# Phi units of a fused retention and two-MoE kernel: loaded in the experts' order, one expert ahead

## The chip, the cores and the metric

One Trainium2 chip, one core, one program. The metric is the device time of one execution in microseconds (us). All data are fp32; the large matrix products run as sums of two reduced parts (fp32r).

## The reference

```python
# attention: B,H,S,D = 4,8,768,64; x is its output as 3072 tokens x 512
for t in range(S):
    state = gamma * state + outer(k[:, :, t], v[:, :, t])
    y[:, :, t] = scale * (q[:, :, t] @ state)
# first MoE: 8 experts, each token goes to one
logits = x @ w_gate;  e_idx = argmax(logits)
gate_w = softmax(logits)[e_idx];  eom = sigmoid(x @ w_output_gate)
for e in range(8):
    mask = e_idx == e
    h = relu(x[mask] @ w1[e])                       # 512 -> 1024
    out[mask] = gate_w[mask] * eom[mask, e] * (h @ w2[e])
# second MoE: soft slots, 8 experts x 4 slots
logits = out @ phi                                  # 3072 x 32
d = softmax(logits, over tokens);  c = softmax(logits, over slots)
slot_in = d.T @ out;  slot_out = expert MLP of each slot
return c @ slot_out                                 # 3072 x 512
```

## The kernel before

The kernel runs as three stages in one hand-written order (the schedule is manual: every engine executes its instructions in the order of the program, and SP's queue issues nearly all loads in that order too).

**First stage** (pool scope `pa`, lines 311 to 757): 24 tiles of 128 tokens (`NTILE`). A loop over i runs the steps named in `ORDER`: score matmuls of tile i+1 (L452), masks on VectorE (L462), output matmuls (L476, L485), state (L499), and for every third tile the gates of three tiles (L535, L550), their choice of expert and their rank. `load(i + 4)` (L420) reads 1 MB of raw q, k, v into a pool of five buffers. `x_put` and `scale_put` (L648, L640) write finished rows and their scales to `xs` in DRAM.

**Phi units.** The logits of the second MoE are needed while the first MoE runs. Instead of multiplying the first MoE's output by phi, the kernel multiplies `w2[e] @ phi` once per expert: 8 experts x 4 units (`NQ` = 32). A unit is 512 KB of w2, 4 matmuls (8 instructions) against a 32-column block of phi (L237); after four units VectorE transposes the block (L407, L1107). Units 0 to 15 run inside the first stage's loop (step `w`), loaded through a pool of four buffers (L377); 16 to 23 run in its tail (`u1`, `u3`, L700), loaded as four 1 MB pieces into the raw buffers (L382); 24 to 31 are loaded at the start of the second stage (L1101) and run in two groups behind its steps 2 and 4. They run in the order of the expert's number, ahead of the time at which it is known in which order the experts are processed, so each finished block goes to DRAM (`wps`, L245) and comes back by the ordered expert's number (L943).

**The turn.** After the last tile, the counts give the order of the experts by size; SP reads the first expert's number (`load_er(0)`) and loads its first weights (L214); the token lists are made (L731), and GpSimd gathers the rows of the first expert from `xs` (L743). Then all engines read a limit and branch over a block for overflowing experts (L857, not entered with these inputs).

**Second stage** (lines 878 to 1222): 64 steps g, expert e = g // 8, part f = g % 8. A step is `l1(g)`, 12 matmuls (L921), with the weights split in two two steps ahead (`split_w`, L223, L224) and loaded three steps ahead (`load_w`, three buffers). `behind(e - 1, f)` places the other work of the previous expert behind the steps: logits (L957), their sum, softmax parts, slot products (L1040, L1062), combine weights (`c_exp`, `c_put`), w2 loads. Rows of the next expert are gathered at f = 0 to 3, scaled at f = 4 and 5, transposed at f = 7 (L899). In free buffers the weights of the second MoE (`m2`) are loaded ahead: 50 of 128 tiles (`NPRE`).

**Third stage** (lines 1225 to 1358): the second MoE on 32 slots: first layer (L1238), second layer in two column halves (L1275, order `ORDC`), then the output as `c @ slot_out`: the first half's columns of all tokens (`emit_out(0)`, parts `o0-4` to `o20-24`), then the second half's (`emit_out(1)`). `combine` (`s`, `S`) finishes a half's sum. Each output DMA writes two tokens' half rows per partition, 1 KB pieces. Remaining m2 tiles are loaded as buffers fall free.

Of the kernel before, what the change touches and what calls it, by code (L numbers as in the profile page):

```python
# [36 lines left out]
NPRE, NX = 50, 4  # L37
NH = 6
NQ = 4 * E
NQL, NQ0 = 16, 24  # L40
# [98 lines left out]
def retention_moe_kernel(ctx, tc, qt, kt, kn, vn, gates, moe_w1, moe_w2,  # L139
# [30 lines left out]
    wps = dr.tile([E, 128, KF * NS], F32, name="wps")  # L170
# [57 lines left out]
    wtt, wacc, wput, wput_old = {}, {}, {}, []  # L228

    def wq_mm(u, pool, tag):  # L230
        if not 0 <= u < NQ:
            return
        e, kk = divmod(u, 4)
        if kk == 0:
            wacc[e] = pool.tile([128, 256], F32, tag=tag, name="wps")
        for g, t in enumerate(wtt.pop(u)):
            nc.tensor.matmul(out=wacc[e][32 * g:32 * g + 32, :], lhsT=phi[:, kk, :], rhs=t,  # L237
                             start=(kk == 0), stop=(kk == KD - 1), skip_group_check=True)

    def wq_put(wait):  # L240
        for e in list(wput):
            if wait and e not in wput_old:
                wput_old.append(e)
                continue
            nc.sync.dma_start(out=wps[e], in_=wput.pop(e).rearrange("p f s -> p (f s)"))  # L245
# [65 lines left out]
    with ExitStack() as pa:  # L311
        sc2 = pa.enter_context(tc.tile_pool(name="sc2", bufs=2))
        io = pa.enter_context(tc.tile_pool(name="io", bufs=5))
# [55 lines left out]

        wst = pa.enter_context(tc.tile_pool(name="wst", bufs=4))  # L370

        def wq_load(i):

            if i % 5 < 4 and i // 5 * 4 + i % 5 < NQL:
                e, q = divmod(i // 5 * 4 + i % 5, 4)
                t = wst.tile([128, FF], F32, tag="wt", name="wt")
                nc.sync.dma_start(out=t, in_=moe_w2[1, e, :, q * FF:(q + 1) * FF])  # L377
                wtt[4 * e + q] = [t[:, g * 256:g * 256 + 256] for g in range(4)]
            elif NTILE - 4 <= i < NTILE:
                e, q = divmod(NQL + 2 * (i + 4 - NTILE), 4)  # L380
                t = io.tile([128, 4 * DM], F32, tag="raw", name="wt2")
                nc.sync.dma_start(out=t, in_=moe_w2[1, e, :, q * FF:(q + 2) * FF])  # L382
                for h in range(2):
                    wtt[4 * e + q + h] = [t[:, h * FF + g * 256:h * FF + g * 256 + 256] for g in range(4)]

        def wq_at(i):
            if 2 <= i < 22 and (i - 2) % 5 < 4:
                return [(i - 2) // 5 * 4 + (i - 2) % 5]
            return []

        def wq_step(i):
            for u in wq_at(i):
                wq_mm(u, pT, "w")
                wq_turn(u)

        wq_end = iter(range(NQL, NQ0))

        def wq_next(n):
            for _ in range(n):
                u = next(wq_end)  # L400
                wq_mm(u, pT, "w" if u < NQL + 4 else "st")

        def wq_turn(u):
            if u % 4 == 3 and 0 <= u < NQ0:

                wput[u // 4] = pd[:, 0:KF, :] if u == NQ0 - 1 else sc2.tile([128, KF, NS], F32, tag="ws", name="ws")
                nc.vector.transpose(out=wput[u // 4], in_=wacc.pop(u // 4).rearrange("p (f t) -> p f t", t=32))  # L407
# [309 lines left out]
        for g in range(3):  # L717
            load_w(g)
# [159 lines left out]
    with ExitStack() as pb:  # L878
# [231 lines left out]
        for u in range(NQ0, NQ0 + 4):  # L1110

            first = wq_early(u)
            if u == NQ0:
                after(first, gets[0])
# [270 lines left out]
```

## Time and profile before

| | us |
|---|---|
| median of three runs | 433.23 (432.98 to 437.45) |
| the profiled execution | 433.41 |
| its span, first to last instruction | 431.6 |
| TensorE (PE) busy | 378.8 (88%) |
| VectorE (DVE) busy | 259.4 (60%) |
| ScalarE (ACT) busy | 161.1 (37%) |
| GpSimd (POOL) busy | 110.0 (25%) |

The DMA engines moved 132.96 MB, 308 GB/s on average. The time beyond the span, 1.8 us, lies around the program. Busy shares are averages over three stages with different limits, so they are read by stage.

### The profile page before, as it was taken

What the parts mean: (1) busy time and instruction counts of PE and PEld (TensorE: products, weight loads), DVE (VectorE), ACT (ScalarE), POOL (GpSimd) and SP (SyncE); (2) the same over time, 40 slices, a digit from 0 to 9 for tenths busy, and PEclk for the clock granted to TensorE, in tenths of its full rate; (3) what the DMA queues carried; (4) which work ended last, traced back from release to release, by engine and by line L of the source; (5) the groups of instructions that cost most, each with busy time, mean ns of one, the idle gap of its engine ahead of it and who ended that gap; (6) DMA issues with size and microseconds to landing.
All of it is one profiled execution on the core that took longest, in us unless ns stands there. A gap on an engine that the chain in (4) does not pass through costs nothing.

```text
span 431.6 us, 11452 instructions
## 1 busy us (share of the span) xinstructions
PE 378.8 (88%) x4398; PEld 285.7 (66%) x4398; DVE 259.4 (60%) x676; ACT 161.1 (37%) x359; POOL 110.0 (25%) x117
## 2 busy tenths in 40 slices
PE   2799998797981999999999999999999996799990
PEld 2776776676750877877897878878788873224560
DVE  1468988589774326658666586675756756414350
ACT  1242222122211237454654646445554441112242
POOL 2223321222113131214324253152431312020020
PEclk9899999899995699999999999999999999899996
DMA  8999999999998797896877958778687688999998
GB/s 268 380 412 321 345 356 345 382 361 340 331 334 219 287 334 275 288 326 195 275 277 257 332 187 293 263 251 301 223 290 244 201 285 292 393 398 404 398 371 285
DMA packets 68290, 132.96 MB, mean 308 GB/s; under 512 B 10660, under 2 KB 31138, under 8 KB 65410
## 3 DMA queue, kind: packets, MB, share of 16 engines
q1 hardware_dynamic: 61442, 120.17, 80.1%
q0 software_dynamic: 3344, 8.34, 5.8%
q10 hardware_dynamic: 3440, 3.63, 2.5%
q8 instruction: 36, 0.59, 0.5%
q14 instruction: 28, 0.23, 0.2%
HBM read 117.89 MB, written 14.25 MB: 306 GB/s over the span
## 4 chain that ended last, share of the span: by engine, by line
PE 63%; DMA 16%; DVE 11%; ACT 3%; issue 2%; another core or an unknown queue 2%; SPq 1%; ACTq 1%; POOL 0%; POOLq 0%; DVEq 0%
PE hps L921 28%; PE gps L1040 5%; PE fh L1238 4%; PE s L452 3%; PE o L485 3%; DMA raw<-in_qt_dram 3%; PE so L1275 3%; DMA r<-in_moe_w_dram 3%; DMA wt<-in_moe_w_dram 3%; PE xps L899 3%; PE slo L1062 2%; PE lps L957 2%; DMA xs<-xr 2%; DMA raw<-in_vn_dram 2%; PE o L476 2%
## 5 line engine op out<-in xcount | busy, mean ns | idle before, releaser
L921 PE MATMUL hps<-xh,wh 128*128 128x416 f32 (+2 forms) x256 | 92.6, 362 | 1.1 <-ACT h L932 1.1
L921 PE MATMUL hps<-xl,wh 128*128 128x416 f32 (+2 forms) x256 | 89.8, 351 | 0.1
L921 PE MATMUL hps<-xh,wl 128*128 128x416 f32 (+2 forms) x256 | 89.6, 350 | 0.0
L224 DVE TENSOR_TENSOR wl<-r,wh 128x512 fp32r<-128x512 f32 x64 | 43.7, 684 | 52.9 <-ACT wh L223 43.8
L921 PEld LDWEIGHTS hps<-xh,wh 128*128 128x128 f32 x256 | 48.7, 190 | 15.2 <-issue 11.2
L932 ACT ACTIVATE h<-hps 128x416 f32<-128x416 f32 (+2 forms) x64 | 32.6, 510 | 68.7 <-PE hps L921 66.4
L1023 POOL DMA_INDIRECT ctok<-ce,xidx x29 | 29.2, 1008 | 88.0 <-DVE ce L1020 81.6
L223 ACT ACTIVATE wh<-r 128x512 fp32r<-128x512 f32 x64 | 40.1, 628 | 26.7 <-DMA r<-in_moe_w_dram 14.3
L921 PEld LDWEIGHTS hps<-xl,wh 128*128 128x128 f32 x256 | 48.8, 190 | 1.4 <-DVE xl L909 0.7
L921 PEld LDWEIGHTS hps<-xh,wl 128*128 128x128 f32 x256 | 48.7, 190 | 0.7
L462 DVE TENSOR_TENSOR sS<-s,csa 128x512 f32<-128x512 f32 x48 | 30.4, 676 | 28.7 <-PE s L452 28.7
L743 POOL DMA_INDIRECT xg<-xs,xidx x29 | 30.3, 1045 | 62.5 <-ACT h L932 50.1
L452 PE MATMUL s<-raw 64*128 64x128 f32 x384 | 31.0, 304 | 12.1 <-DMA raw<-in_qt_dram 10.2
L452 PEld LDWEIGHTS s<-raw 64*128 64x128 f32 x384 | 26.0, 204 | 14.6 <-DMA raw<-in_qt_dram 5.8
L939 DVE STREAM_TRANSPOSE hB<-h 128x416 f32<-128x416 f32 (+2 forms) x64 | 34.4, 577 | 0.0
L517 ACT COPY xT<-o 128x512 f32<-128x512 f32 x24 | 13.9, 580 | 43.4 <-PE o L485 43.4
L434 POOL TENSOR_TENSOR k<-raw,cs 128x512 f32<-128x512 f32 x20 | 21.7, 1091 | 30.3 <-DMA raw<-in_qt_dram 18.9
L485 PE MATMUL o<-sS,raw 128*64 128x128 f32 x384 | 28.5, 295 | 0.0
L485 PEld LDWEIGHTS o<-sS,raw 128*64 128x64 f32 x384 | 22.3, 145 | 3.9 <-issue 3.6
L1040 PE MATMUL gps<-hB,pd 32*32 32x256 f32 x816 | 20.4, 412 | 3.7 <-DVE pd L994 3.7
L899 PE MATMUL xps<-cs,xg 128*128 128x128 f32 (+2 forms) x116 | 15.6, 284 | 9.0 <-DVE xg L890 9.0
L970 POOL TENSOR_SCALAR msk<-cs,rt 128x416 f32<-128x416 f32 (+2 forms) x8 | 15.8, 1972 | 25.2 <-DVE srun L996 23.6
(175 smaller groups left out, 529.0 us busy)
## 6 DMA issues: line engine op xcount, KB each, us to landing
m<-in_moe_w_dram SPq DMA_DIRECT2D x41, 512.0 KB
r<-in_moe_w_dram SPq DMA_DIRECT2D x64, 256.0 KB
w<-in_moe_w_dram SPq DMA_DIRECT2D x64, 256.0 KB
m<-in_moe_w_dram SPq DMA_DIRECT2D x36, 256.0 KB
wt<-in_moe_w_dram SPq DMA_DIRECT2D x16, 512.0 KB
xs<-xr SPq DMA_DIRECT2D x32, 192.0 KB
raw<-in_kt_dram SPq DMA_DIRECT2D x5, 1024.0 KB
raw<-in_kn_dram SPq DMA_DIRECT2D x5, 1024.0 KB
```

What stands on the lines that cost most here:

```text
L223: nc.scalar.activation(out=hi, in_=t, func=ACTF.Copy)
L224: nc.vector.tensor_tensor(out=lo, in0=t, in1=hi, op=ALU.subtract)
L452: nc.tensor.matmul(out=ps[h][:, p, :], lhsT=kq(i, p, 0)[r], rhs=kq(i, p, 1)[r], start=True, stop=True, tile_position=(64 * h, 0), skip_gro ...
L462: nc.vector.tensor_tensor(out=sS[i][:, h], in0=sps.pop((i, h)), in1=con("dm", 128)[:, 4 * h:4 * h + 4, :], op=ALU.mult)
L485: nc.tensor.matmul(out=o_at(i, p, h), lhsT=vals(i, 2 * p + h), rhs=s[:, h, p, :], start=(i % NCH == 0 and n < 4), stop=True, skip_group_ch ...
L743: gets.setdefault(e, []).append(nc.gpsimd.indirect_dma_start(out=t[0:r, :], out_offset=None, in_=xs[:, :], in_offset=bass.IndirectOffsetOn ...
L899: nc.tensor.transpose(out=ps[kk][:, j * 128:j * 128 + r], in_=xg[e][j][0:r, kk * 128:(kk + 1) * 128], identity=ident[0:r, 0:r])
L921: nc.tensor.matmul(out=ps, lhsT=a[:, kk * 128:(kk + 1) * 128], rhs=x[e][kk][:, 0:c], start=(n == 0), stop=(n == 11))
L932: relu.append(nc.scalar.activation(out=hs[g][:, 0:c], in_=ps, func=ACTF.Relu))
L939: nc.vector.transpose(out=hB[e][:, 0:NB[e], f, :], in_=hs[e * KF + f][:, 0:c].rearrange("p (b t) -> p b t", t=32))
L1023: put = nc.gpsimd.indirect_dma_start(out=ctok[:, :], out_offset=bass.IndirectOffsetOnAxis(ap=xidx[0:r, e, j:j + 1], axis=0), in_=cn[0:r, j ...
L1040: nc.tensor.matmul(out=ps[a][32 * j:32 * j + 32, :], lhsT=pd[q, b, :], rhs=hB[e][q, b].rearrange("p f t -> p (f t)"), start=(i == 0), stop ...
```

## The change

- Phi units are loaded by the order of the experts (`er[k]`) and never leave the chip: no `wps`, no L245, no L943. The first expert's four units are loaded (two pieces of 1 MB) after its first weights and run, as one group of 32 matmul instructions, at the end of the first stage, with their transpose, ahead of the branch. The second expert's are loaded when its predecessor's rows have been gathered, into a new pool `wup` of four buffers. For every later expert: expert e + 1's group runs behind step f = 2 (f = 4 for e = 0), and expert e + 2's units are loaded at the three steps after it.
- The first stage has no units, seven raw buffers instead of five, and loads six tiles ahead.
- `NPRE` goes from 50 to 42; eight more m2 tiles go into `wup` near the end of the second stage.
- Gathers at f = 1 to 4 and the scalings at f = 5 and 6, one step later each; `c_exp` and `c_put` one step sooner.
- The last step: the second last expert's `slot_in` and eight m2 loads come before the last logits.
- Output: tokens 14 to 23 of each partition as whole rows after both halves' sums (`emit_rows`), tokens 0 to 13 as before.

```diff
-NPRE, NX = 50, 4
+NPRE, NX = 42, 4
+IO, UMM = 6, 2
-ORDER = "xe sc s m g1 gc xr w rr g2 G0 Gb q oq os st G1 rk k".split()
+ORDER = "xe sc s m g1 gc xr rr g2 G0 Gb q oq os st G1 rk k".split()
-ORDER_24 = "xe u1 g1 gc u1 xr g2 G0 u3".split()
+ORDER_24 = "xe g1 gc xr g2 G0".split()
-ORDC = "p 00 01 02 03 t 04 05 06 07 c s 10 11 o0-4 12 o4-8 13 o8-12 14 15 o12-16 16 17 d o16-20 S o20-24".split()
+ORDC = "p 00 01 02 03 t 04 05 06 07 c s 10 11 o0-4 12 o4-8 13 o8-12 14 15 o12-14 16 17 d S".split()
...
+    def wq_load(k, q, n, pool, tag):
+        t = pool.tile([128, n * FF], F32, tag=tag, name="wt")
+        get = nc.sync.dma_start(out=t, in_=moe_w2[1, bass.ds(er[k], 1), :, q * FF:(q + n) * FF].rearrange("o p d -> (o p) d"))
+        for h in range(n):
+            wtt[k, q + h] = [t[:, h * FF + g * 256:h * FF + g * 256 + 256] for g in range(4)]
+        return get
+
+    def wq_mm(k, pool, tag):
+        wacc[k] = pool.tile([128, 256], F32, tag=tag, name="wps")
+        for q in range(KD):
+            for g, t in enumerate(wtt.pop((k, q))):
+                nc.tensor.matmul(out=wacc[k][32 * g:32 * g + 32, :], lhsT=phi[:, q, :], rhs=t,
+                                 start=(q == 0), stop=(q == KD - 1), skip_group_check=True)
+
+    def wq_turn(k, out):
+        wp[k] = out
+        nc.vector.transpose(out=out, in_=wacc.pop(k).rearrange("p (f t) -> p f t", t=32))
...
-        io = pa.enter_context(tc.tile_pool(name="io", bufs=5))
+        io = pa.enter_context(tc.tile_pool(name="io", bufs=IO + 1))
...
-        wst = pa.enter_context(tc.tile_pool(name="wst", bufs=4))
...
-            wq_put(1)
-            wq_load(i)
-            load(i + 4)
+            load(i + IO)
...
         load_er(0)
         for g in range(3):
             load_w(g)
+        for q in range(0, KD, 2):
+            wq_load(0, q, 2, io, "raw")
         rank(i)
...
-        wq_turn(NQL + 3)
-        wq_put(0)
+        wq_mm(0, pT, "w")
         lx = one.tile([128, E, 4, E], F32, name="lx")
...
         lists(slice(1, E))
-        wq_turn(NQ0 - 1)
+        wq_turn(0, pd[:, 0:KF, :])
...
+    wup = ctx.enter_context(tc.tile_pool(name="wup", bufs=KD))
...
-            if e + 1 < E and f < len(XT[e + 1]):
-                gather(e + 1, (f,))
+            if e + 1 < E and 0 < f <= len(XT[e + 1]):
+                gather(e + 1, (f - 1,))
...
-            if f in (4, 5) and e + 1 < E:
+            if f in (5, 6) and e + 1 < E:
...
             behind(e - 1, f)
-            if e == 0 and f in (2, 4):
-                wq_late(NQ0 // 4 + f // 2 - 1)
+            if g == G - 1:
+                slot_in(e - 1)
+                for _ in range(8):
+                    load_m2(w2p, "w2")
+            u = UMM if e else UMM + 2
+            if f == u and e + 1 < E:
+                wq_mm(e + 1, ps_1, "A")
+                wq_turn(e + 1, sp.tile([128, KF, NS], F32, tag="wp", name="wp", bufs=2))
+            if f > u and f <= u + 3 and e + 2 < E:
+                for q in ((0, 1), (2,), (3,))[f - u - 1]:
+                    wq_load(e + 2, q, 1, wup, "wu")
+            elif G - 14 < g < G - 6 and f % 2:
+                load_m2(wup, "wu", 2)
...
+        def emit_rows(lo, hi):
+            i = lo
+            while i < hi:
+                at = next((at for at in spots if at[0] and at[2] == 2), None)
+                if at:
+                    spots.remove(at)
+                    t, w = at[0].tile([128, 2 * 512], F32, tag=at[1], name="ot"), 2
+                else:
+                    (t, at), w = spare([128, 512], "ot"), 1
+                for j in range(w):
+                    ps = ps_c.tile([128, 512], F32, tag="c", name="ops")
+                    nc.tensor.matmul(out=ps, lhsT=cT_t[(i + j) // 4][:, (i + j) % 4, :], rhs=s3[0], start=True, stop=True)
+                    (nc.scalar.copy if (i + j) % 2 else nc.vector.tensor_copy)(out=t[:, j * 512:j * 512 + 512], in_=ps)
+                (nc.scalar if i // 2 % 2 else nc.sync).dma_start(
+                    out=out.rearrange("(p i) d -> p i d", p=128)[:, i:i + w, :].rearrange("p i d -> p (i d)"), in_=t)
+                spots.append(at)
+                i += w
...
-        emit_out(1)
+        emit_rows(14, NTILE)
+        emit_out(1, 0, 14)
```

## Rows read from the trace of the kernel before

**Rows 1.** The page's slices: tenths busy in 40 equal slices of the span.

```profile
PE   2799998797981999999999999999999996799990
...
DMA  8999999999998797896877958778687688999998
```

**Rows 2.** Windows, three tiles each: length, busy us by engine, clock, DMA share, GB/s.

```profile
25.67:38.67 13.00, 12.57 (x224) 9.57 (x220) 10.93 (x33) 4.25 (x13) 3.44 (x5) 1.00 0.96 370
38.67:51.21 12.54, 11.94 (x215) 9.46 (x213) 10.62 (x33) 3.45 (x9) 3.73 (x6) 1.00 0.97 329
51.21:64.39 13.18, 12.00 (x216) 9.44 (x213) 11.30 (x33) 3.68 (x10) 3.58 (x4) 1.00 1.04 361
...
sum 84.03, PE 75.10 PEld 58.88 DVE 67.54 ACT 20.85 POOL 22.36; mean PE 12.52 PEld 9.81 DVE 11.26 ACT 3.48 POOL 3.73
```

**Rows 3.** Timeline of PE, first stage: start, us, line, operands, [idle before].

```profile
44.57 0.64 PE L237 MATMUL wps<-wt,phi 128*32 128x256 f32 x8
45.14 0.18 PE L609 MATMUL g<-oh,tri 128*128 128x8 bf16 x1
...
52.97 0.61 PE L237 MATMUL wps<-wt,phi 128*32 128x256 f32 x8
53.75 0.84 PE L550 MATMUL g<-csa,gsb 128*128 128x16 f32 x6 [0.17 <-ACT gsb L543]
...
64.39 1.16 PE L452 MATMUL s<-raw 64*128 64x128 f32 x16 [1.02 <-DMA raw<-in_kn_dram]
```

**Rows 4.** Timeline of SP's queue, the end of the first stage.

```profile
125.61 3.82 SPq L648 DMA_DIRECT2D xs<-xr  x4
129.53 0.96 SPq L640 DMA_DIRECT2D xs<-sv  x1
132.12 1.46 SPq L214 DMA_DIRECT2D r<-in_moe_w_dram  x3
```

**Rows 5.** Timeline of DVE, from the last gates to the first expert.

```profile
128.02 0.45 DVE L600 RECIPROCAL sv<-sm 128x48 f32<-128x48 f32 x1
...
139.15 0.69 DVE L224 TENSOR_TENSOR wl<-r,wh 128x512 fp32r<-128x512 f32 x1
141.32 0.49 DVE L890 TENSOR_SCALAR xg<-xg 128x512 f32<-128x512 f32 x1 [1.47 <-DMA xg<-xs,xidx]
```

**Rows 6.** Line 857, the branch: count, min/median/max ns, first and last start.

```profile
L857 DVEq EVENT_SEMAPHORE  x2: 21/21/21, 137.5 to 137.6; - x2
...
L857 PEldq COMPARE_BRANCH  x1: 4438/4438/4438, 133.1 to 133.1; - x1
L857 DVEq COMPARE_BRANCH  x1: 72/72/72, 133.4 to 133.4; - x1
```

**Rows 7.** Windows: the turn, the first expert, the other seven.

```profile
130.90:143.04 12.14, 3.16 (x12) 2.15 (x13) 4.05 (x15) 1.89 (x4) 3.76 (x4) 0.50 0.66 181
143.04:170.66 27.62, 26.56 (x185) 22.07 (x185) 10.74 (x20) 12.37 (x25) 6.23 (x6) 0.92 0.87 317
...
170.66:361.70 191.04, 189.47 (x1787) 151.43 (x1784) 127.25 (x295) 98.25 (x210) 62.41 (x54) 1.00 0.79 265
```

**Rows 8.** Timeline of PE: four Phi units in the second stage.

```profile
151.74 1.93 PE L237 MATMUL wps<-wte,phi 128*32 128x256 f32 x32
153.61 0.44 PE L921 MATMUL hps<-xh,wh 128*128 128x384 f32 x1
```

**Rows 9.** Windows: one expert of the second stage, and 3 us of it.

```profile
228.60:256.30 27.70, 27.56 (x262) 22.21 (x258) 18.46 (x43) 14.82 (x32) 10.43 (x10) 1.00 0.79 267
...
244.00:247.00 3.00, 3.00 (x17) 2.98 (x17) 0.69 (x2) 0.89 (x3) 0.00 (x0) 1.00 1.05 392
```

**Rows 10.** Windows of the third stage; waits of PE in the second.

```profile
376.00:380.00 4.00, 3.98 (x24) 1.14 (x28) 1.65 (x6) 0.31 (x1) 1.77 (x2) 0.57 1.05 401
...
422.00:424.00 2.00, 0.00 (x0) 0.00 (x0) 0.00 (x0) 1.12 (x2) 0.00 (x0) 1.00 1.02 348
...
PE lsum L978 <- DVE ll L965: 1.2, 3, 0.6
```

More of the change, by code (lines that the diff above doesn't have):

```diff
@@ L225, in split_w @@
         w1_t[g] = (hi, lo)
[L228 to L245, printed above, removed]
+    wtt, wacc, wp = {}, {}, {}
+    def wq_load(k, q, n, pool, tag):
[13 more added lines that the diff above has]
+        nc.vector.transpose(out=out, in_=wacc.pop(k).rearrange("p (f t) -> p f t", t=32))
     def m2_src(n, w):
@@ L368, in decay_table @@
                                          scale=dc[:, c - 2, q:q + 1])
-        wst = pa.enter_context(tc.tile_pool(name="wst", bufs=4))
[L372 to L407, printed above, removed]
         raw, k2, q2, sps, sS, Ops, xT3, xr3, gps, gts, gs, scl, gr, oz = ({} for _ in range(14))
@@ L668, in retention_moe_kernel @@
         late_consts(1)
-        load(3)
+        for i in range(3, IO):
+            load(i)
         k_scale(0)
@@ L881, in retention_moe_kernel @@
         ps_1 = pb.enter_context(tc.tile_pool(name="ps_1", bufs=1, space=PSUM))
-        xh, xl, hs, hB, wp, w2n, lps, lrs, lrs2, sms, msks, lms, ces, gps, gts, grs, slo = ({} for _ in range(17))
-        puts, pair, relu = {}, [], []
+        xh, xl, hs, hB, w2n, lps, lrs, lrs2, sms, msks, lms, ces, gps, gts, grs, slo = ({} for _ in range(16))
+        puts, relu = {}, []
         def x_scale(e, j, vector=False):
@@ L1086, in behind @@
                 c_tr(e)
+                c_exp(e)
             elif f == 5:
                 slot_s(e)
-                c_exp(e)
+                c_put(e)
             elif f == 6:
                 slot_t(e)
-                c_put(e)
             if 2 < f < 7:
                 load_w2(e, (2 * f - 6, 2 * f - 5))
-        def wq_early(u):
-            e, q = divmod(u, 4)
-            t = m2p.tile([128, FF], F32, tag="m2", name="wte")
-            wtt[u] = [t[:, g * 256:g * 256 + 256] for g in range(4)]
-            return nc.sync.dma_start(out=t, in_=moe_w2[1, e, :, q * FF:(q + 1) * FF])
-        def wq_late(e):
-            for u in range(4 * e, 4 * e + 4):
-                wq_mm(u, ps_1, "r")
-            ws = wput[e] = sp.tile([128, KF, NS], F32, tag="wp", name="ws", bufs=2)
-            nc.vector.transpose(out=ws, in_=wacc.pop(e).rearrange("p (f t) -> p f t", t=32))
-        wq_put(0)
[L1110 to L1114, printed above, removed]
+        load_er(1)
+        for q in range(KD):
+            get = wq_load(1, q, 1, wup, "wu")
+            if q == 0:
+                after(get, gets[0])
         for j in range(len(XT[0])):
@@ L1152, in retention_moe_kernel @@
                 load_m2(m2p, "m2", 2)
[L1153 to L1154 removed]
+            if f in (5, 6) and e + 1 < E:
+                for j in range(2 * f - 10, min(2 * f - 8, len(XT[e + 1]))):
                     x_scale(e + 1, j)
@@ L1190, in retention_moe_kernel @@
             load_m2(xtp, "xl")
-        for _ in range(8):
-            load_m2(w2p, "w2")
         h_tr(e, 6)
```

32 lines of the change are left out of this document (4 added, 28 removed).

## The prediction

> **What bounds the kernel now.** I read the page's slices first. TensorE (PE) is the only engine near full, and the DMA engines are full in two stretches: the first 130 us and the last 70 [rows 1]. So the kernel has three stages with different limits, and the change moves work from the first to the second.
>
> *First stage* (the 24 token tiles, to about 130 us). The windows between the score matmuls of every third tile show how long three tiles take: 12.5 us where nothing is late, and 84.0 for six such groups, 14.0 on average [rows 2]. The DMA share is 0.96 to 1.04 [rows 2], so loads come late; in the undisturbed group PE is busy 11.94 and VectorE (DVE) 10.62 of 12.54 us [rows 2]. The floor is PE, with DVE close under it.
>
> *Second stage* (64 first-layer steps). PE is busy 189.47 of 191.04 us from the second expert to the end, with DMA at 0.79 [rows 7]. Any matmul added here is paid in full.
>
> *Between them* (130.9 to 143.0) the chain of waits holds no matmul that limits: the last scales are written to xs, the first expert's rows are gathered, every engine takes a branch, and rows are scaled, turned and split [rows 4 to 6].
>
> **Part 1: the first stage loses 24 Phi units.** Sixteen ran inside the loop, eight in its tail. One unit is 8 matmul instructions, 0.64 us busy, and moves the next matmul back 0.57 [rows 3]. Where it stands behind the gate matmul it fills a wait: the gate's second matmul still waits 0.17 for ScalarE (ACT) [rows 3]; the order of the steps puts it there about every third time. The undisturbed group holds two units that are exposed: 12.54 - 2 x 0.57 = 11.4. The next one holds one, and a wait of 1.02 for raw data: 13.18 - 0.57 - 1.02 = 11.6 [rows 2, 3]. Would DMA still be late? By the sizes in the code 12.6 of some 38 MB of loads go, beside 7 MB of writes; a share of about 1.0 over 130 us falls to some 0.8 over 115, and seven buffers instead of five reach further ahead. I take the waits for loads as gone. Six groups: 6 x 11.5 + 0.7 for the decay tables in the first = 69.7 against 84.0, and one exposed unit before them: -14.9. PE and DVE are then nearly equal (11.4 against 10.6), which costs something where they alternate: I take **-14.5**. Bounds: -15.5 (no coupling) and -11 (each group at 12.1). The eight units in the tail stand where PE waits for DVE: 0.
>
> **Part 2: the turn from stage one to two.** Now the first expert's four units are loaded after its number is known, and multiplied *before* the branch. In program order PE has that group ahead of the branch and of the row transposes; DVE has its transpose ahead of the branch and of the row scaling. Both wait for 2 MB.
> - The last scales are ready at 128.02 + 0.45 = 128.5; SP issued their write only at 129.53, being in row writes from 125.61 on [rows 4, 5]. With the queue empty it issues at 128.5. The weight loads followed 2.6 us later [rows 4]: 131.1, and take 1.46; the two 1 MB loads stand at 132.6.
> - Bytes: 0.79 MB of weights, 2.10 of units, 0.81 of gathered rows. At 401 GB/s, what plain loads reach [rows 10], all of it takes 9.2 us; at 317, the mean of loads and gathers at the start of stage two [rows 7], 11.7. From 131.6 that ends between 140.8 and 143.3; I take 142.0. Lower bound, with the gathers taking no share: 2.9 MB at 401, 138.8.
> - The last two units (16 instructions) run at the granted clock of this gap, 0.50, the lower level of 1.2 GHz [rows 7]: half of the 32 instructions that took 1.93 at the upper [rows 8], doubled: 1.9. The transpose 0.4, an estimate beside 0.49 for a row scaling of twice the columns: 144.3.
> - The branch: PE's took 4.44 us; DVE branched at 133.4 and went on at 137.5, 4.1 later [rows 6]. In the kernel before these ran beside the gather. Now both start behind the group: 148.7.
> - Two row scalings of 0.49 with one weight split of 0.69 between, then 1.2 to the first layer-one matmul (141.81 to 143.04) [rows 5, 7]: 151.6.
>
> Against 143.04: **+8.6**, bounds +5.4 and +11. The Trainium skill ("Runtime: NRT & Kernel Launch", Instruction fetch mechanics) says that a taken branch to code outside the fetched window stalls until a DMA has brought it; the trace agrees, at 4.1 to 4.4 us. The Trainium skill's page "Advanced Engine Details and Errata" (Control Flow Timing) puts a compare-and-branch at about 108 ns; by that alone the turn would cost 4 us less. The row decides here.
>
> **Part 3: stage two gains Phi groups.** Four units together are 32 instructions, 1.93 busy, next matmul 1.87 us behind their start; with the first weights of the matmul that follows, 1.95 [rows 8]. Before, the first expert's steps held two groups; now one. Experts two to seven each hold one, none before: 6 x 1.95 = **+11.7**. PE has no idle time there [rows 7] that could hide it. The first expert: -1.95, and of its 1.06 idle (27.62 - 26.56 [rows 7]) 0.9, since the weights no longer queue behind 4 MB of units: **-2.85**.
>
> The five more DVE transposes, the gathers issued one step later (GpSimd's queue, with their scalings one step later on ACT) and the combine weights one step sooner (DVE and GpSimd) cost nothing: PE's 99% hides them [rows 7]. Without that cover a transpose costs its 0.4 an expert, and rows that come too late a step, some 3.4 us (191.04 over 56 steps). The trips of the finished Phi blocks through DRAM (16 transfers of 128 KB) vanish from SP's queue, worth nothing on the path either.
>
> **Part 4: DMA in stage two.** Per expert it moved 267 GB/s x 27.7 us = 7.4 MB at share 0.79 [rows 9]; now 2.1 MB more in 29.6 us: 321 GB/s, where 1.0 would be 267/0.79 = 338. That is 0.95 on average, and it is uneven: already now 3 us of each expert stand at 1.05 [rows 9], and three steps in a row will ask for units, w2 and m2 together. SP's unit load waits for the Phi group on PE; behind it in SP's queue are the next weight loads, which split_w and through it PE need. Two to three steps of lead cover that. I take **+1**; bounds 0 and +5.
>
> **Part 5: the end.** The second-layer product of expert six now runs before the last logits, so the split of those logits loses its cover; the same wait was up to 0.6 where cover was thin [rows 10]: +0.6. The eight early m2 tiles wait for that product, so they are hardly sooner. Output: the DMA engines are full to the end; loads in 4 KB rows run at 401 GB/s, the output in 1 KB pieces at 348 [rows 10]. Ten tokens' 2.6 MB as 2 to 4 KB rows would gain up to 0.9 if writes follow that. But three output pairs no longer come before the second half's sum, so the engines run dry for some 2 us. **+1.5** in all; bounds -1.5 and +2.5.
>
> **Sum.** -14.5 + 8.6 - 2.85 + 11.7 + 1 + 1.5 = +5.45. The profiled execution took 433.41 (span 431.6, 1.8 around it), 0.2 from the median of 433.23. 433.4 + 5.45 = **438.9 us**.
>
> **Rivals.**
> 1. *The exchange pays: faster.* Deciding point: the first Phi group's place. If its 2 MB land and its transpose is done by 136, before the gathered rows, the turn costs nothing and gains the 1.1 us by which the scales go out sooner; with the first stage at its good bound, 438.9 - 8.6 - 1.1 - 1.0 = 428.2. For it: the DMA engines have room there (share 0.66 [rows 7]). Against it: the weight loads can't be issued before 131, and 2.9 MB need 7.2 us: the data alone come at 138.8.
> 2. *No change.* The branch costs nothing when it comes late, its code being fetched while PE and DVE wait: 438.9 - 4.4 = 434.5; with the first stage at its good bound 433.5. For it: the waits for loads would leave time. Against it: PE and DVE each show the stall after their own branch, at different times [rows 6]. The Trainium skill's page "Advanced Engine Details and Errata" (Control Flow Timing), named above, speaks for this one.
> 3. *Late weights: much slower.* If 0.95 is too full, each of the five experts with all four streams waits 2 us for weights: 438.9 + 10 = 449. For it: the 1.05 stretch [rows 9]; against: the lead of two to three steps.
> 4. *The change does not do what it says* (units still early, or hidden): the diff excludes it, since the program order is kept.
>
> **How the numbers follow.** A measurement of this kernel can tell about 1% from no change, so 428.9 and 437.6 divide. The forecast (437.6 to 444): 0.42. Late weights: 0.10. No change: 0.32. Faster: 0.16. Faster 0.16, same 0.32, slower 0.52. The likeliest case's own range is 435 to 444. Range for 8 in 10: from 429, which takes in rival 2 and leaves out most of rival 1, to 447, which takes in half of rival 3.
>
> **What would show it.** Six groups of three tiles in some 70 us with no wait for raw; from the last list matmul to the first layer-one matmul 12.1 + 8.6 = 20.7 us, in which PE waits for Phi data and DVE's branch follows its transpose; PE's stage from the second expert on 11 to 13 us longer, with DMA at 0.9 or more; 1 to 2 us more behind the last second-layer matmul. I am wrong if the turn takes under 15 us, if PE idles over 6 us in stage two, or if three tiles still take over 12.5.

## The result, and the profile after

The changed kernel is slower. Its median is 441.83 us (438.78 to 446.48, six runs); that of the kernel before is 437.06 (432.98 to 438.74, six runs, the three of the table above among them). The ratio, taken from the fast runs alone (446.48 is a slow one), is 1.0129, with a 95% interval of 1.0082 to 1.0175; on the 433.23 us of the table above that is 438.8 (436.8 to 440.8), where the prediction was 438.9. A second session gave 1.0158 (1.0096 to 1.0220).

The profiled execution took 443.59 us, 10.2 more than that of before. That overstates the change: 433.41 lies near the low end of the runs of before, 443.59 above the median of the changed kernel. The traces are good for *where*, the ratio for *how much*. All stretches below are read from PE's timelines. The list matmul is the last one of the first stage; a `so` product is one of the second MoE's second layer, and behind the last of them only the output is left.

| stretch | before | after | difference | predicted |
|---|---|---|---|---|
| start to the last list matmul (L686) | 130.83 | 116.42 | -14.41 | -14.5 |
| turn: to the first layer-one matmul | 12.21 | 25.65 | +13.44 | +8.6 |
| first expert | 27.62 | 22.87 | -4.75 | -2.85 |
| experts two to eight | 187.86 | 199.67 | +11.81 | +12.7 |
| last layer-one matmul to last `so` product | 56.46 | 59.43 | +2.97 | +0.6 (split of the logits) |
| to the end | 16.66 | 17.76 | +1.10 | +0.9 (rest of the end) |
| span | 431.64 | 441.81 | +10.17 | +5.45 |

The page's slices after, to be held against [rows 1]:

```profile
PE   3889999997133999999999999999999996799980
...
PEclk9999999999555999999999999999999997699996
DMA  8999999944646698978979989989688687999988
```

PE's slices 11 to 13 (about 110 to 143 us) are the hole that takes the gain back; in the same slices the granted clock is at the lower level.

Windows after, three tiles each (length, busy us of PE, PEld, DVE, ACT and POOL, clock, DMA share, GB/s), against [rows 2]:

```profile
35.71:47.44 11.73, 10.86 (x198) 9.14 (x196) 10.05 (x31) 3.44 (x9) 3.45 (x6) 1.00 1.01 330
47.44:59.16 11.72, 11.12 (x201) 9.19 (x197) 10.71 (x33) 3.09 (x9) 3.38 (x5) 1.00 1.00 315
...
sum 71.85, PE 66.63 PEld 55.38 DVE 63.08 ACT 20.21 POOL 21.96; mean PE 11.10 PEld 9.23 DVE 10.51 ACT 3.37 POOL 3.66
```

Six groups take 71.85 us instead of 84.03, and no group waits long for data: PE's waits for raw data are 0.7 us in all, where the kernel before has 6.2 us of waits for loads. PE is busy 93% of the time (66.63 of 71.85), before 89% (75.10 of 84.03).

The turn after, on PE's timeline, and the two-microsecond windows of the load in it:

```profile
126.23 1.94 PE L241 MATMUL wps<-wt,phi 128*32 128x256 f32 x16 [9.80 <-SPq L818]
130.53 1.94 PE L241 MATMUL wps<-wt,phi 128*32 128x256 f32 x16 [2.37 <-SPq L818]
139.22 2.79 PE L861 MATMUL xps<-cs,xg 128*128 128x128 f32 x12 [6.75 <-DVE xg L852]
142.07 0.69 PE L883 MATMUL hps<-xh,wh 128*128 128x384 f32 x1
```

```profile
124.00:126.00 2.00, 0.00 (x0) 0.00 (x0) 0.00 (x0) 0.00 (x0) 0.00 (x0) 0.50 1.02 422
126.00:128.00 2.00, 1.77 (x16) 0.59 (x16) 0.00 (x0) 1.24 (x2) 0.00 (x0) 0.50 0.43 174
128.00:130.00 2.00, 0.16 (x4) 0.00 (x0) 0.00 (x0) 0.00 (x0) 0.00 (x0) 0.50 0.05 18
130.00:132.00 2.00, 1.47 (x16) 0.60 (x16) 0.00 (x0) 0.00 (x0) 0.00 (x0) 0.50 0.00 0
```

PE waits three times: 9.80 us for the first MB of units, 2.37 for the second, 6.75 for the first expert's scaled rows. The releaser named for the first two is SP's semaphore at the branch; by the code these matmuls wait only for their data. (`wps` is the sum of a Phi group, `xps` the transposes of an expert's rows, `hps` the first layer.) On DVE's timeline and at the branch (L818) the second half of the story stands:

```profile
132.53 0.45 DVE L246 STREAM_TRANSPOSE pd<-wps 128x256 f32<-128x256 f32 x1 [13.79 <-PE wps L241]
138.47 0.49 DVE L852 TENSOR_SCALAR xg<-xg 128x512 f32<-128x512 f32 x1 [5.49 <-DVEq L818]
```

```profile
L818 PEldq COMPARE_BRANCH  x1: 3552/3552/3552, 131.2 to 131.2; - x1
```

DVE comes to the branch only behind its transpose, and stands 5.49 us before it scales the first row. PE's own branch took 3.55 us. PE and DVE branch 12 to 15 us after ScalarE, GpSimd and SP (118.6 to 118.9), and still stand: 3.55 us on PE against 4.44 in [rows 6], and 5.1 from DVE's branch to its next instruction (133.2 to 138.3) against 4.1 there.

Stage two and three after, as windows: the first expert, experts two to eight, to the third stage's first matmul, to the last product, the end:

```profile
142.07:164.94 22.87, 22.86 (x153) 20.73 (x154) 11.01 (x20) 13.03 (x26) 5.53 (x5) 0.94 0.77 259
164.94:364.61 199.67, 198.55 (x1955) 155.41 (x1958) 128.66 (x298) 95.91 (x207) 60.88 (x55) 1.00 0.86 297
364.61:383.96 19.35, 12.20 (x155) 4.55 (x154) 8.00 (x25) 2.78 (x8) 0.15 (x1) 0.73 0.89 310
383.96:424.04 40.08, 39.14 (x440) 17.54 (x440) 12.10 (x45) 8.26 (x19) 4.55 (x5) 0.96 1.04 395
424.04:441.80 17.76, 6.09 (x27) 3.94 (x26) 6.16 (x10) 5.24 (x10) 0.00 (x0) 0.81 0.81 292
```

### The profile page after: what moved, and what is told of

It reads as the page before. It is cut to its first block, busy times and chain, and to the rows that moved or that the text cites. A ratio compares the mean times of both kernels' runs of the same rounds, so it can differ in the third digit from the quotient of the medians.

```text
span 441.8 us, 11442 instructions
## 1 busy us (share of the span) xinstructions
PE 380.1 (86%) x4388; PEld 284.1 (64%) x4388; DVE 258.5 (59%) x677; ACT 159.5 (36%) x358; POOL 106.2 (24%) x115
## 4 chain that ended last, share of the span: by engine, by line
PE 54%; DMA 8%; DVE 3%; ACT 1%; issue 1%; ACTq 0%; SPq 0%
PE hps L883 31%; PE gps L992 4%; PE slo L1014 4%; DMA m<-in_moe_w_dram 3%; PE xps L861 3%; PE wps L241 3%; PE lps L909 3%; PE so L1213 3%; DMA r<-in_moe_w_dram 2%; DMA two<-ctok 1%; DMA w<-in_moe_w_dram 1%; PE gsum L1005 1%; PE lsum L930 1%; PE ops L1271 1%; DVE ot L1290 1%
## 5 line engine op out<-in xcount | busy, mean ns | idle before, releaser
L241 PE MATMUL wps<-wt,phi 128*32 128x256 f32 x256 | 17.4, 414 | 12.2 <-SPq L818 12.2
L447 PE MATMUL o<-sS,raw 128*64 128x128 f32 x384 | 27.1, 285 | 0.0
L447 PEld LDWEIGHTS o<-sS,raw 128*64 128x64 f32 x384 | 21.2, 140 | 3.7 <-issue 3.3
```

The lines of the kernel that those rows point to most:

```text
L241: nc.tensor.matmul(out=wacc[k][32 * g:32 * g + 32, :], lhsT=phi[:, q, :], rhs=t, start=(q == 0), stop=(q == KD - 1), skip_group_check=True)
L447: nc.tensor.matmul(out=o_at(i, p, h), lhsT=vals(i, 2 * p + h), rhs=s[:, h, p, :], start=(i % NCH == 0 and n < 4), stop=True, skip_group_ch ...
```

## The experiments

Each experiment changes the changed kernel, unless it says otherwise. The first four ran on one chip, the next four on another, the next three on a third, the last one alone; the ratio is always to the kernel before on the same chip. The stretches of all traces, in us:

| kernel | ratio (95%) | last list matmul | turn | first expert | two to eight | to last `so` | end |
|---|---|---|---|---|---|---|---|
| before | 1 | 130.83 | 12.21 | 27.62 | 187.86 | 56.46 | 16.66 |
| changed | 1.0129 (1.0082 to 1.0175) | 116.42 | 25.65 | 22.87 | 199.67 | 59.43 | 17.76 |
| changed, again | 1.0158 (1.0096 to 1.0220) | 116.22 | 21.57 | 22.38 | 200.95 | 59.38 | 17.74 |
| own step | 1.0028 (0.9988 to 1.0067) | 116.64 | 11.06 | 26.41 | 202.84 | 58.33 | 17.90 |
| behind the branch | 1.0080 (1.0044 to 1.0115) | 118.09 | 16.28 | 24.05 | 200.26 | 58.98 | 18.11 |
| old output | 1.0114 (1.0060 to 1.0168) | 116.45 | 24.60 | 22.41 | 199.15 | 58.43 | 16.68 |
| no products | 0.9912 (0.9877 to 0.9946) | 117.47 | 24.75 | 20.86 | 187.09 | 61.30 | 17.75 |
| no unit loads | 1.0134 (1.0093 to 1.0175) | 117.36 | 22.12 | 22.33 | 196.73 | 61.23 | 17.70 |
| products alone in stage one | 1.0282 (1.0237 to 1.0327) | 120.79 | 21.28 | 22.28 | 201.11 | 59.98 | 17.76 |
| order alone | 0.9956 (0.9928 to 0.9983) | 118.87 | 11.34 | 23.81 | 199.60 | 60.46 | 16.68 |
| old slot place | 1.0142 (1.0072 to 1.0212) | 116.05 | 21.19 | 21.84 | 197.91 | 56.12 | 17.75 |
| old gathers | 1.0140 (1.0088 to 1.0193) | 116.86 | 25.56 | 22.65 | 197.36 | 58.69 | 17.74 |
| order alone 2 | 0.9933 (0.9892 to 0.9974) | 116.47 | 11.19 | 24.16 | 199.62 | 56.13 | 16.70 |
| three undone | 1.0082 (1.0046 to 1.0118) | 116.47 | 24.07 | 22.82 | 196.81 | 56.23 | 16.69 |

**The changed kernel again**, no edit.

> The changed kernel itself, unaltered, as the yardstick on the same chip as the three kernels beside it. Both theories: 1.010 to 1.016 of the kernel before. In its trace the first stage's last list matmul should end 14 us earlier than before, the first layer-one matmul come 25 to 26 us after it (12.2 before), the first expert take 22.9 us (27.6 before), and experts two to eight 199 to 200 us (187.7 before).

1.0158, and the stretches as expected but for the turn, 21.57 us instead of 25.65. Over the nine traces with the group ahead of the branch the turn lies between 21.2 and 25.7, 23.4 on average: +11.2 against before.

**Own step.**

```diff
-        for q in range(0, KD, 2):
-            wq_load(0, q, 2, io, "raw")
-        wq_mm(0, pT, "w")
-        wq_turn(0, pd[:, 0:KF, :])
-            get = wq_load(1, q, 1, wup, "wu")
+            get = wq_load(0, q, 1, wup, "wu")
...
-            if f == u and e + 1 < E:
-                wq_mm(e + 1, ps_1, "A")
+            if f == u:                   # u = 2 for every e
+                wq_mm(e, ps_1, "A")
...
-                    wq_load(e + 2, q, 1, wup, "wu")
+                    wq_load(e + 1, q, 1, wup, "wu")
...
```

The four buffers are in use longer, so the eight m2 tiles that go into them are loaded at steps 59 to 62 instead of 51 to 57.

> One part of the change moved: each expert's four Phi units are loaded during the expert ahead, but multiplied in step 2 of the expert's own run, two steps before the logits that want them. Nothing of Phi then stands ahead of the branch at the turn; expert one's units are loaded where the change loads expert two's. Theory 'the loss is the turn' (2 MB and then the code fetch, one behind the other): the first layer-one matmul comes 11 to 13 us after the last list matmul instead of 25.6 (-13 or so), one more Phi group runs at stage two's clock (+2): the whole 10 to 12 us faster than the changed kernel, 1 to 1.5% faster than the kernel before. Rival 'the data are late wherever they are wanted': the 4 loads are awaited in step 2 instead, PE waits some 8 us there, and the time moves by less than 3 us. Rival 'the loss is stage two': the turn is hidden by other lateness and the time moves by less than 3 us.

PE's timeline of the turn, and the windows of the first expert and of the others:

```profile
124.84 2.79 PE L857 MATMUL xps<-cs,xg 128*128 128x128 f32 x12 [8.20 <-DVE xg L848]
127.70 0.69 PE L879 MATMUL hps<-xh,wh 128*128 128x384 f32 x1
```

```profile
127.70:154.11 26.41, 24.59 (x152) 21.68 (x153) 11.45 (x20) 13.09 (x26) 5.53 (x5) 0.90 0.92 333
154.11:356.95 202.84, 200.50 (x1987) 156.48 (x1990) 129.65 (x298) 96.77 (x207) 61.63 (x55) 1.00 0.85 299
```

The turn is 11.06 us: 10.5 to 14.6 gained, as the first theory had it, and nothing is awaited in step 2. But only 1.3% of time came of it (1.0028 against 1.0158), not over 2%: the first expert takes 3.5 to 4 us more. It holds one Phi group here as in the changed kernel, so that is not the reason. PE stood idle for 1.82 us (26.41 less 24.59), nearly all of it at the second expert's transposes, for rows scaled late; behind this wait the granted clock is 0.58 from 150.00 to 154.11 us, which by 4.11 x 0.42 is worth another 1.7. Experts two to eight hold one group more, 1.95. So the loss is the turn, and a second cost stood behind it.

**Behind the branch.**

```diff
-IO, UMM = 6, 2
+IO, UMM = 4, 2
-        for q in range(0, KD, 2):
-            wq_load(0, q, 2, io, "raw")
+        for q in range(KD):
+            wq_load(0, q, 1, wup, "wu")      # wup now stands ahead of the first stage
-        wq_mm(0, pT, "w")
-        wq_turn(0, pd[:, 0:KF, :])
...
         load_er(1)                           # behind the branch
+        wq_mm(0, ps_1, "r")
...
             x_split(0, ps)
+        wq_turn(0, pd[:, 0:KF, :])
```

> Tells the two terms of the turn apart. Expert one's four units are still loaded at the same place (into the four buffers that stage two uses, for which the loads of the first stage go only four tiles ahead instead of six), but multiplied behind the branch, ahead of the transposes of the first expert's tokens, which still wait for them in TensorE's order. Theory 'wait and code fetch add up': the engines take the branch 10 us earlier, its fetch lies under the load, and the first layer-one matmul comes 5 to 7 us earlier than in the changed kernel (19 to 20 us after the last list matmul): 5 to 7 us off the time. Rival 'a branch that comes late costs nothing' (only the load counts): the first layer-one matmul stays within 1.5 us of the changed kernel's, and so does the time. Fewer tiles ahead should cost the first stage under 1 us by either.

The branch (L817), and PE's timeline:

```profile
L817 PEldq COMPARE_BRANCH  x1: 6794/6794/6794, 120.3 to 120.3; - x1
L817 DVEq COMPARE_BRANCH  x1: 72/72/72, 120.7 to 120.7; - x1
```

```profile
128.16 2.79 PE L241 MATMUL wps<-wt,phi 128*32 128x256 f32 x24 [10.08 <-SPq L817]
131.41 1.08 PE L241 MATMUL wps<-wt,phi 128*32 128x256 f32 x8 [0.45 <-SPq L817]
132.42 1.57 PE L859 MATMUL xps<-cs,xg 128*128 128x128 f32 x12
134.37 0.44 PE L881 MATMUL hps<-xh,wh 128*128 128x384 f32 x1 [0.38 <-ACT xh L868]
```

The units come no sooner: the last one's products start 13.3 us after the last list matmul (14.1 in the changed kernel). But the branch lies under their load, DVE scales meanwhile, and the transposes follow at once: the turn is 16.28 us, 4.9 to 9.4 less, and the time falls by some 3.4 us (1.0080 against 1.0158). Wait and fetch add up where the group stands ahead of the branch. The loads four tiles ahead instead of six made the first stage 1.7 us longer, more than expected.

**Old output.**

```diff
-ORDC = "... o12-14 16 17 d S".split()
+ORDC = "... o12-16 16 17 d o16-20 S o20-24".split()
-        emit_rows(14, NTILE)
-        emit_out(1, 0, 14)
+        emit_out(1)
```

> Only the output's order undone: all 24 tokens' first halves go out before and between the last products, all 24 second halves behind them, as in the kernel before; everything else as changed. Theory (whole rows save fewer eviction starts than the later first halves cost): 1 us faster than the changed kernel, from the end's 17.8 us between the last product and the last write down to 16.7. Rival (the row writes save the 0.9 us that fewer evictions take): 1 us slower.

In the traces the end is 16.66 to 16.70 in all five kernels that keep the old order, before included, and 17.70 to 18.11 in the other nine. That is the expected 1 us; by the ratios alone (1.0114 against 1.0158) the two can't be told apart.

**No products.**

```diff
-                wq_mm(e + 1, ps_1, "A")
-                wq_turn(e + 1, sp.tile([128, KF, NS], F32, tag="wp", name="wp", bufs=2))
+                wp[e + 1] = wp[0]
```

> The price of the Phi groups on TensorE in stage two: the changed kernel without the matrix products of experts two to eight's units (their logits take expert one's factors, so that part of the computation is left out; the loads stay). Theory 'TensorE is the bound there, the loads are hidden': experts two to eight take 187.5 to 189 us instead of 199 to 201, the first expert 2 us less, and the time falls by 13 to 14 us against the changed kernel (ratio to the kernel before 0.98 to 0.99). Rival 'the loads are late' (the data pace stage two): the products' room fills with waits for r, xg or w, and the time falls by less than 6 us.

```profile
163.09:350.18 187.09, 185.95 (x1763) 149.96 (x1766) 126.31 (x293) 95.23 (x207) 60.62 (x55) 1.00 0.90 320
350.18:367.77 17.59, 10.34 (x154) 4.31 (x154) 8.01 (x25) 2.79 (x8) 0.16 (x1) 0.89 0.88 308
367.77:411.48 43.71, 39.65 (x440) 17.80 (x440) 12.13 (x45) 8.15 (x19) 4.55 (x5) 0.93 1.02 386
```

Six executions with the products and the gathers of the changed kernel lie between 197.9 and 201.1 us in experts two to eight, 199.8 on average; without the products it is 187.09, 12.7 less: PE is the bound there. The time fell by 2.2 to 2.5%, some 10 us, less than expected, and the table shows where it went: the stretch to the last product grew to 61.30. There the DMA share is 1.02: the second MoE's weights set the pace, and by the longer stretch they come no sooner for the sooner end of stage two.

**No unit loads.**

```diff
-            for g, t in enumerate(wtt.pop((k, q))):
+            for g, t in enumerate(wtt[min(k, 1), q]):
-                    wq_load(e + 2, q, 1, wup, "wu")
+                    pass
```

> The price of the unit loads in stage two: the changed kernel without the loads of experts three to eight's units (12 MB less; their products are made, but from expert two's units, so that part of the computation is left out). Theory 'the loads are hidden': experts two to eight stay within 1 us of the changed kernel's 199 to 201 us, the third stage too, and the time falls by 0 to 1.5 us (ratio 1.010 to 1.016). Rival 'late weights': 5 to 10 us faster.

```profile
161.81:358.54 196.73, 196.73 (x1955) 155.59 (x1958) 129.41 (x298) 96.30 (x207) 62.39 (x55) 1.00 0.74 246
```

PE without any idle time, and 196.73 us instead of 199.8 on average: by this trace the loads cost some 3 us (1.2 against the shortest of the six), between the two theories. In the time nothing of it arrives (1.0134): again the third stage takes it, 61.23.

**Products alone in stage one.**

```diff
+        def dummy(i):                        # step "w", for i from 2 to 21
+            ps = pT.tile([128, 256], F32, tag="w", name="dps")
+            for n in range(4):
+                nc.tensor.matmul(out=ps[32 * n:32 * n + 32, :], lhsT=phi[:, n, :], rhs=dq[0][:, n % 2, :],
+                                 start=True, stop=True, skip_group_check=True)
```

> Whether the first stage's gain came from TensorE or from the loads: the changed kernel with four products of a unit's size in each of twenty steps of the first stage, at the place where the kernel before made its units, from a table that is resident (no load; their result is not used). Theory 'TensorE is the bound of that stage': its groups of three tiles go from 12.0 back to 13.5 to 14.0 us, the last list matmul comes 11 to 13 us later than in the changed kernel, and the time is 11 to 13 us above it (ratio 1.037 to 1.046). Rival 'the units' loads held the stage up': under 3 us later.

```profile
36.73:49.27 12.54, 12.37 (x223) 9.72 (x221) 10.47 (x32) 3.45 (x9) 3.68 (x6) 1.00 0.99 327
...
sum 75.94, PE 74.67 PEld 57.87 DVE 64.11 ACT 20.52 POOL 22.76; mean PE 12.45 PEld 9.65 DVE 10.69 ACT 3.42 POOL 3.79
```

Neither theory: six groups take 75.94 us. Eighteen units add 8.04 us of work on PE (74.67 less 66.63) and 4.09 to the length, 0.23 a unit; the rest fills waits, most of them for ScalarE (in the changed kernel PE waits eight times for it at L512, 4.8 us in all). The other 8.09 up to the 84.03 of before go mostly with the loads. In the kernel before they show in the last three groups, which [rows 2] leave out, and in what PE waited for there:

```profile
64.39:81.35 16.96, 13.43 (x220) 10.59 (x220) 11.88 (x32) 3.10 (x8) 5.19 (x6) 0.94 1.03 365
81.35:95.02 13.67, 12.66 (x215) 10.11 (x213) 10.76 (x32) 3.51 (x9) 2.21 (x5) 0.95 1.04 356
95.02:109.70 14.68, 12.50 (x220) 9.71 (x220) 12.05 (x33) 2.86 (x8) 4.21 (x5) 1.00 1.02 350
```

```profile
PE wps L237 <- DMA wt<-in_moe_w_dram: 4.4, 2, 2.8
```

With 1.8 us for raw data that is 6.2 us of waits for loads, and the granted clocks of 0.94 and 0.95 in the first two of these groups are worth some 1.7 more (16.96 x 0.06 and 13.67 x 0.05). Not all of it need be the units' own loads: the changed kernel also reaches six tiles ahead instead of four, which is worth up to 1.7 us of the first stage (behind the branch), and the unit blocks' transposes and writes are gone too.

**Order alone**: own step, the old output, and the gathers a step sooner.

```diff
-            if e + 1 < E and 0 < f <= len(XT[e + 1]):
-                gather(e + 1, (f - 1,))
+            if e + 1 < E and f < len(XT[e + 1]):
+                gather(e + 1, (f,))
...
-            if f in (5, 6) and e + 1 < E:
+            if f in (4, 5) and e + 1 < E:
```

> The own-step kernel with two more parts of the change undone: the output's order as before, and the gathers of the next expert's tokens and their scaling a step sooner, as before. What is left of the change is the units loaded by the experts' order and the combine weights a step sooner. Theory: the output gives 1 us, and the 1.8 us that TensorE waited for the second expert's scaled tokens in the own-step kernel go: 2 to 3 us faster than that one, 0.3 to 0.7% faster than the kernel before. Rival (the wait came from the loads' order, not from the gathers' step): within 1.2 us of the own-step kernel.

0.9956 (0.9928 to 0.9983): faster than the kernel before. The first expert and the others fell by 2.6 and 3.2 us against own step, more than the one wait of 1.8 that the trace had shown; of the 0.7% between the two ratios the output is 1 us.

**Old slot place.**

```diff
-            if g == G - 1:
-                slot_in(e - 1)
-                for _ in range(8):
-                    load_m2(w2p, "w2")
...
         logit_parts(e)
+        slot_in(e - 1)
...
             load_m2(xtp, "xl")
+        for _ in range(8):
+            load_m2(w2p, "w2")
```

> One part of the change undone: the second-layer product of expert seven and the eight m2 loads that reuse its buffers go back behind the last logits, the loads behind the ten that reuse layer-one's buffers. In the traces of the changed kernel SP's queue stands at these eight loads until that product is done, and the DMA share is 0.00 to 0.02 in the 2 us after the last layer-one matmul (0.89 before), 0.85 to 0.89 from there to the third stage's first matmul (1.00 before), while the third stage is paced by the m2 loads. Theory 'the blocked queue is paid in the third stage': the share right after layer one is back over 0.85, the stretch from the last layer-one matmul to the last product is 56 to 57.5 us instead of 58.3 to 59.4, and the time falls by 2 to 3 us, with 0.85 us of waits for the logits' split among it. Rival 'only the cover of the logits' split was lost' (the loads come no sooner, as the prediction had it): 0.6 to 0.9 us.

The first 2 us behind the last layer-one matmul, and from there to the third stage's first matmul:

```profile
356.99:358.99 2.00, 2.00 (x20) 0.94 (x23) 0.07 (x2) 0.98 (x2) 0.17 (x1) 1.00 0.87 287
356.99:372.77 15.78, 9.44 (x154) 4.21 (x155) 8.05 (x25) 2.79 (x8) 0.17 (x1) 1.00 0.97 341
```

The same 2 us in the changed kernel:

```profile
364.61:366.61 2.00, 2.00 (x22) 0.61 (x24) 0.05 (x1) 0.49 (x1) 0.15 (x1) 1.00 0.00 1
```

The trace says the first theory: the queue is no longer blocked, and the stretch to the last product is 56.12 us, below before's. All three kernels with the old place have 56.1 to 56.2, the ten with the new one 58.3 to 61.3. The time doesn't show it: 1.0142, with an interval wide enough to hide 3 us (the runs lay between 432.6 and 442.7).

**Old gathers**, the last edit of order alone by itself.

> One part of the change undone: the gathers of the next expert's tokens and their scaling go back a step. Theory 'TensorE's cover hides a gather that comes a step later' (the prediction's): no difference over 0.5 us in experts two to eight, the time within 1 us. Rival, from the own-step kernel, whose experts two to eight went from 202.8 to 199.6 us with the gathers a step sooner: 1.5 to 3 us faster, with the transposes xps at 268 ns a piece instead of 271 and their waits of 0.4 to 0.9 us gone.

```profile
165.07:362.43 197.36, 197.36 (x1955) 155.48 (x1958) 129.22 (x298) 96.82 (x207) 60.89 (x54) 1.00 0.87 301
```

197.36 us with no idle time of PE, and the transposes at 268 ns: the rival's signs, 2.4 us under the average of 199.8 (196.81 in three undone, below). The size is loose: old slot place, with the late gathers, has 197.91, 0.5 us of idle time and the transposes at 268 ns too. The ratio, 1.0140, is the changed kernel's; the trace has a turn of 25.56, which would hide the gain.

**Order alone 2**: order alone with the old slot place.

> The order-alone kernel with the second-layer product and its eight loads put back too. What is left of the change is the units loaded by the experts' order, each expert's multiplied in its own step 2, and the combine weights a step sooner. Theory: 2 to 3 us faster than the order-alone kernel (0.9956 of the kernel before), so 0.989 to 0.992 of the kernel before. Rival (the third stage gives it back): 0.994 to 0.996.

0.9933 (0.9892 to 0.9974), the fastest of all, within what the rival allows too. In the trace the stretch to the last product went from 60.46 to 56.13.

**Three undone**: old output, old gathers and old slot place, the look-ahead kept.

> The three small parts undone together, the look-ahead kept: output order, gathers' step and second-layer product's place as before, the Phi units by the experts' order with expert one's still ahead of the branch. One by one each was worth less than its measurement's uncertainty. Theory 'each is worth about what its trace showed' (1.1 at the end, 1.5 to 3 in experts two to eight, 2 to 3 in the third stage): 4 to 6 us faster than the changed kernel, 1.000 to 1.006 of the kernel before; what is left against the own-step kernel with the same three undone (0.993) is the turn, some 4 us. Rival 'none of the three is worth anything, the turn is all': 1.012 to 1.016, as the changed kernel.

1.0082, between the two: the three together are worth 0.5 to 0.8%, some 2 to 3 us, where the traces add up to over 6. The difference to order alone 2, which differs by the own step alone, is 1.5% (6.4 us); the two traces differ by 8.8: -12.9 in the turn, +1.3 in the first expert, +2.8 behind it.

## Why the prediction was right, and where not

The time came out as forecast, and the mechanism of its main term is the one that the runs show. Of its terms, several were off, and some cancelled.

- **Part 1, -14.5; measured -14.41.** Right in sum, wrong in its split. The six groups gained 12.18, not 14.3: they take 11.97 each, near the worse bound of 12.1, not 11.5. And the step "the floor is PE" failed: a unit on PE is worth 0.23 us there, not the 0.57 by which it moves the next matmul [rows 3], since it fills waits far oftener than every third time. Up to two thirds of the gain (8.09 of 12.18) go with the loads. The missing 2.4 us is a start that differs by execution: the score matmul at 25.67 in [rows 2] stands at 23.28 after, at 22.9 to 24.3 in nine of the other ten executions of this stage, and at 25.68 in order alone, where PE waited 3.05 us for raw data before a score matmul at 17.74, with the granted clock at 0.50 right behind. The trace of before has the same low clock there (0.50 from 18 to 20 us), so this much need not be the change; with one trace of before it is not shown.
- **Part 2, +8.6; measured +13.4 in this trace, +9.0 to +13.4 in nine, +11.2 on average.** The mechanism (2 MB, then the branch, one behind the other) is shown by own step and behind the branch; the landing was mis-sized. To the end of DVE's transpose 16.6 us passed, not 13.5: the bytes moved at the rate assumed (395 to 422 GB/s from 120 to 126 us), but the second MB was usable only at 130.53, when the DMA share had been at 0.05 for 2 us. The trace marks the landing of such a load sixteen times. In the nine traces the eighth mark of the second MB comes 10.1 to 10.9 us after the last list matmul, where the prediction had the whole at 11.2; the sixteenth comes at 10.7 to 14.8, and the turn goes with it (21.19 us at 10.7, 25.65 at 14.1, 25.56 at 14.8). The branch cost DVE 5.5 here and 3.8 to 5.6 in the nine, 4.5 on average, beside the 4.4 forecast; the rest was 3.6 in all nine, not 2.9. Rival 2, the late branch that costs nothing, falls: 3.33 to 3.77 us on PE in all nine. The Trainium skill's figure ("Advanced Engine Details and Errata", Control Flow Timing) of about 108 ns holds for no engine's first instruction behind this branch.
- **First expert, -2.85; measured -4.75.** The missing group is in it, and the wait for weights is gone (0.01 us idle). Of the rest, 1.75 us of PE's busy time, about half goes with the clock: 0.94 in this window, 0.92 in [rows 7] (27.62 x 0.08 less 22.87 x 0.06 is 0.8). It is not that PE had just run the Phi group: in own step, which has none there, the clock is at 0.98 from 2 us after the first layer-one matmul.
- **Part 3, +11.7, with nothing for the gathers.** The price of a group was right: PE is busier by 12.3 us for six groups in the windows (198.55 less 186.29 in before), and without them the stretch falls by 12.7. "Later gathers cost nothing" failed, as did the cover named for it: by the traces they cost 2.4 to 3 us against the average (old gathers, three undone), and 0.5 in the one of old slot place. The prediction's own price of rows too late, some 3.4 us in one expert, was the right size for the sum.
- **Part 4, +1; measured some 3** (no unit loads). It is the same 3 us as the gathers': taking away either, the loads or the late step, brings the stretch to 196.7 to 197.4 with PE never idle. By these traces the rows come late only because both fall together. That the two parts still came out within 0.9 us has a reason that the prediction did not list: the 1.2 us of waits for the logits' split [rows 10] are gone from this stretch. Rival 3, late weights, had no part: no wait for the weights or their split halves stands in PE's list.
- **Part 5, +1.5; measured +4.1.** The output's part was right (+0.9 expected, +1.1 found), and so was the split of the logits (0.6 expected, PE waits 0.7 and 0.2 us for it, and not at all with the old slot place). The step that failed is "the eight early m2 tiles are hardly sooner", costed at nothing. They are the *first* in SP's queue, and everything behind them stands until `slot_in` has freed their buffers: the DMA share is 0.00 for 2 us, at the head of a stage that DMA paces. The prediction did not apply its own question, what is queued behind the waiting instruction.
- **The sum.** That the ratio gives 5.6 us where 5.45 was forecast is in part luck. Part 1 was right by luck; Parts 2 and 5 were too small by 4.8 and 2.6, the first expert's gain by 1.9, Parts 3 and 4 together too large by 0.9; in the two traces that makes 10.2. The changed kernel's second trace is 6.6 us longer than that of before, with 4.1 us less in the turn, and its ratio makes 6.8 of 433.23. Which stretches make up the 5.6 to 6.8 of the ratios, single traces can't say. Why single parts show 1 to 3 us in a trace and less in the ratios stays open; executions of one kernel differ by 1 to 2%, and each trace is one of them.

## What to carry to other kernels

Work that waits for a load should not stand ahead of a branch in program order, where everything after it starts behind the branch, as it did here: put it at the last step that still feeds its reader, and the load and the code fetch run side by side. Before you price a step by its time on the busiest engine, put the work back without its loads: here most of what looked like matrix time went with the transfers. And a load issued early into a buffer that is not free yet is no early load: it is a stopped queue.

## What the runs showed of the hardware

- The stall at a taken branch depends on what else moves: on PE 4.44 us before [rows 6], 4.23 beside the first weights and rows alone (own step), 6.79 under 2 MB of loads (behind the branch), 3.55 alone and late (changed). In each of these four stalls the trace lists one transfer of 16 KB on an instruction queue. It starts 1.96, 1.81, 4.28 and 1.20 us after the branch, and PE goes on 1.3 to 1.4 us after its end. That a fetch from memory stands behind it is what the Trainium skill says ("Runtime: NRT & Kernel Launch", Instruction fetch mechanics); the runs agree, in that every stall holds such a transfer, and that the stall is longest beside the loads, where the transfer starts latest.
- The last part of a large load came late: the DMA share was 0.05 and then 0.00 over 128 to 132 us, and the matmuls on the second MB began at 130.53. Of its sixteen landing marks, fourteen stand by 127.04 us, the others at 128.47 and 130.49; the first MB's, fourteen by 123.29, the others at 124.69 and 126.18. The last pieces moved one or two at a time, and transfers of an instruction queue stand among them. A share of 0.05 would fit a single one of the 16 DMA engines that is still behind; the trace does not name the engine, so that is not shown. With four pieces of 512 KB instead of two of 1 MB, three quarters could be used at once and the last quarter 3.25 us after (behind the branch).
